# A 128-column stationary operand for attention times value, in a kernel of cosine attention and a highway layer

## The chip, the cores and the metric

The kernel runs on one NeuronCore of one Trainium2 chip. The metric is the device time of one execution in microseconds, the median of the runs shown. A profile of one execution comes with it; its span runs from the first to the last instruction.

## What is computed

Inputs are q, k and v of shape (8, 12, 448, 64) in fp32: 8 batches, 12 heads, 448 positions, 64 columns. Attention is by cosine: q and k are divided by their norms.

```python
scores = np.matmul(q_n, k_n.transpose(0, 1, 3, 2)) / tau      # tau = 0.1
attn = softmax(scores)
attn_out = np.matmul(attn, v)
x = attn_out.transpose(0, 2, 1, 3).reshape(3584, 768)
H = np.maximum(x @ w_h, 0.0)
T = 1.0 / (1.0 + np.exp(-(x @ w_t + b_t)))
out = T * H + (1.0 - T) * x
```

## The kernel before

S = 448 positions are cut into NC = 4 chunks of P = 112, so most tiles use 112 of 128 partitions. Everything is written for one batch at a time, with pairs of heads (NPAIR = 6) as the unit of loading.

**Preparing a pair.** `emit_A` loads q and k of two heads (L92) through the SyncE queue, squares them on GpSimd (`qk_sq`, L97) and sums the squares on VectorE (L104). `emit_rsqrt` makes the inverse norms on VectorE. `emit_B` multiplies q and k by them on GpSimd (`qkn`, L152, two instructions a pair), transposes the result on TensorE (`qkT`, L157, eight transposes of 112x128 blocks, so the stationary operand is 128 columns wide and the moving identity 112), copies the transposes to SBUF on VectorE (L164), loads v (L168), writes the column of twos that gives the softmax's sum (a GpSimd memset of 112x8, L173) and converts v to fp16 on ScalarE (L174). `vp` is 65 columns wide per head: 64 of v and that one.

**Scores.** `emit_qkt(b, pr, g)` multiplies k chunks by q for two heads at a time (L186, 64 rows, 448 moving columns) into PSUM and takes the exponential on ScalarE (L194, 112x896) into `expt`. Called for g = 0 and 1, it fills, for each head, a tile `expt` of [128, 4, 448] fp16: chunk jc of the keys lies on the partitions, the 448 queries along the row. The pool of `expt` has four buffers, one a head.

**Attention times value.** `emit_av(b, h)` (L201 to L227) makes, for each of four query chunks ic, four accumulating matmuls over jc (L208): the stationary operand is `expt[:P, jc, ic*P:(ic+1)*P]`, 112x112, the moving one `vp[:P, jc, hh]`, 112x65, the output `u[:P, ic, 0:65]` in PSUM. That is 16 pairs of weight load and matmul a head, 96 heads, 1536 pairs. VectorE then takes the reciprocal of the sums (L219) and scales the rows into `xb` (L220).

**The highway layer of the batch before** is spread over the heads of the present one by `ffn_slot`: TensorE transposes `xb` (`xTp`, L234, also with 128-column stationary operands), VectorE copies (L240), TensorE multiplies with w_h and w_t (`pt`, L255, 112-column stationary operand and 384 moving columns) and adds the bias (L263), ScalarE takes tanh (L271), VectorE combines (L274, L291, L299), and SyncE's queue stores the output (L307).

**Order.** The kernel is written with a tile framework. The lines say which engine does what; the framework orders each engine's instructions at compile time by a priority that follows the order of the program (some copies out of PSUM are moved ahead by 300), places tiles in the pools' buffers and sets the semaphores. Each engine then runs its list in order. In the main loop (L330 to L347), head h of batch b comes with the loads of pair h of batch b+1 for h below 6, with the two `expt` tiles and the scores for even h, then `emit_av`, then a slot of the highway layer of b-1, then `emit_B` of batch b+1 for h from 6 on. All of batch 0 is prepared ahead of the loop, and the last batch's highway layer follows it.

Of the kernel before, what the change touches and what calls it, by code (L numbers as in the profile page):

```python
# [10 lines left out]
FP16 = mybir.dt.float16  # L11
# [7 lines left out]
def kernel(  # L19
# [11 lines left out]
    nc = tc.nc  # L31

    B, NH, S, D = q.shape
    P = 112
    NC = S // P
# [17 lines left out]
    expt_p = ctx.enter_context(tc.tile_pool(name="expt", bufs=4))  # L53
# [33 lines left out]
    st = {}  # L87

    def emit_A(b, pr):
        qk_raw = qkraw_p.tile([128, 2, NC, 2, D], FP32, name="qk_raw")  # L90
        for t, src in enumerate((q, k)):
            nc.sync.dma_start(  # L92
                qk_raw[:P, t],
                src[b, 2 * pr : 2 * pr + 2].rearrange("h (p c) d -> p c h d", c=NC),
            )
        qk_sq = qksq_p.tile([128, 2, NC, 2, D], FP16, name="qk_sq")
        nc.gpsimd.tensor_mul(qk_sq[:P], qk_raw[:P], qk_raw[:P])  # L97

        if pr == 0:
            n2 = nrm_p.tile([128, NPAIR, 2, NC, 2], FP16, name="n2")  # L100
            st["n2", b] = n2
        n2 = st["n2", b]
        with nc.allow_low_precision(reason="norm^2 in fp16 (rel err 5e-4)"):
            nc.vector.reduce_sum(n2[:P, pr], qk_sq[:P], axis=AX.X)  # L104
        st["qk_raw", b, pr] = qk_raw

    def emit_rsqrt(b, prs=None):
        n2 = st["n2", b]
        NE = NPAIR * 2 * NC * 2
        if prs is None:  # L110
            if ("rs", b) not in st:
                st["rs", b] = nrm_p.tile([128, NE], FP32, name="yy")
            x32 = nrm_p.tile([128, NE], FP32, name="x32")
            yy = st["rs", b]
            tt_ = nrm_p.tile([128, NE], FP32, name="tt_")
            n2s = n2[:P].opt()
        else:
            if ("rs", b) not in st:
                st["rs", b] = nrm_p.tile([128, NE], FP32, name="yy")
            NE = 16  # L120
            x32 = nrm_p.tile([128, NE], FP32, name="x32p")
            yy = st["rs", b][:, prs * 16 : (prs + 1) * 16]
            tt_ = nrm_p.tile([128, NE], FP32, name="tt_p")
            n2s = n2[:P, prs].opt()
        nc.vector.tensor_copy(x32[:P], n2s)
        nc.vector.tensor_single_scalar(
            yy[:P].bitcast(I32), x32[:P].bitcast(I32), 1, ALU.arith_shift_right
        )
        nc.vector.tensor_scalar(
            out=yy[:P].bitcast(I32),  # L130
            in0=yy[:P].bitcast(I32),
            scalar1=-1.0,
            scalar2=float(0x5F3759DF),
            op0=ALU.mult,
            op1=ALU.add,
        )
        for _ in range(2):
            nc.vector.tensor_mul(tt_[:P], yy[:P], yy[:P])
            nc.vector.tensor_mul(tt_[:P], tt_[:P], x32[:P])
            nc.vector.tensor_scalar(  # L140
                out=tt_[:P], in0=tt_[:P], scalar1=-0.5, scalar2=1.5,
                op0=ALU.mult, op1=ALU.add,
            )
            nc.vector.tensor_mul(yy[:P], yy[:P], tt_[:P])  # L144

    def emit_B(b, pr):
        qk_raw = st.pop(("qk_raw", b, pr))
        rs = st["rs", b].rearrange("p (pr t c h) -> p pr t c h", pr=NPAIR, t=2, c=NC)
        qkn = qkn_p.tile([128, 2, NC, 2, D], FP16, name="qkn")
        for t in range(2):  # L150
            in1 = rs[:P, pr, t].unsqueeze(3).to_broadcast([P, NC, 2, D])
            nc.gpsimd.tensor_mul(qkn[:P, t], qk_raw[:P, t], in1)  # L152

        qkT = pb1_p.tile([128, 2, 512], FP16, name="qkT", tag="pb1")
        for t in range(2):
            for c in range(NC):
                nc.tensor.transpose(  # L157
                    qkT[:, t, c * P : (c + 1) * P],
                    qkn[:P, t, c],
                    ident[:P, :P],  # L160
                )
        qkt = qt_p.tile([128, 2, S], FP16, name="qkt")
        with tc.high_priority(offset=300):
            nc.vector.tensor_copy(qkt[:, :, :], qkT[:, :, 0:S])  # L164
        st["qkt", b, pr] = qkt

        v_raw = vraw_p.tile([128, NC, 2, D], FP32, name="v_raw")
        nc.sync.dma_start(  # L168
            v_raw[:P],
            v[b, 2 * pr : 2 * pr + 2].rearrange("h (p c) d -> p c h d", c=NC),  # L170
        )
        vp = vp_p.tile([128, NC, 2, D + 1], FP16, name="vp")
        nc.gpsimd.memset(vp[:P, :, :, D], 2.0)  # L173
        nc.scalar.copy(vp[:P, :, :, 0:D], v_raw[:P])  # L174
        st["vp", b, pr] = vp

    def emit_qkt(b, pr, g):
        qkt = st["qkt", b, pr]
        sTs = []
        for hh in range(2):  # L180
            sT = sT_p.tile([128, 2, 512], FP32, name="sT", tag="sT")
            sTs.append(sT)
        for jj in range(2):
            jc = 2 * g + jj
            for hh in range(2):
                nc.tensor.matmul(  # L186
                    sTs[hh][:P, jj, 0:S],
                    lhsT=qkt[hh * D : (hh + 1) * D, 1, jc * P : (jc + 1) * P],
                    rhs=qkt[hh * D : (hh + 1) * D, 0, 0:S],
                    start=True,  # L190
                    stop=True,
                )
        for hh in range(2):
            nc.scalar.activation(  # L194
                st["expt", b, 2 * pr + hh][:P, 2 * g : 2 * g + 2, :],
                sTs[hh][:P, :, 0:S],
                AF.Exp,
                scale=inv_tau,
            )

    def emit_av(b, h):  # L201
        pr, hh = h // 2, h % 2
        vp = st["vp", b, pr]
        expt = st["expt", b, h]
        u = pb1_p.tile([128, NC, 128], FP32, name="u", tag="pb1")
        for ic in range(NC):
            for jc in range(NC):
                nc.tensor.matmul(  # L208
                    u[:P, ic, 0 : D + 1],
                    lhsT=expt[:P, jc, ic * P : (ic + 1) * P],  # L210
                    rhs=vp[:P, jc, hh],
                    start=(jc == 0),
                    stop=(jc == NC - 1),
                )

        xb = st["xb", b]
        with tc.high_priority(offset=300):
            rd = nrm_p.tile([128, NC], FP32, name="rd")
            nc.vector.reciprocal(rd[:P, :], u[:P, :, D])  # L219
            nc.vector.scalar_tensor_tensor(  # L220
                out=xb[:P, pr, :, hh, :],
                in0=u[:P, :, 0:D],
                scalar=0.0,
                in1=rd[:P, :].unsqueeze(2).to_broadcast([P, NC, D]),
                op0=ALU.bypass,
                op1=ALU.mult,
            )  # L227
# [81 lines left out]
    def new_batch_tiles(b):  # L309
        xb = xb_p.tile([128, NPAIR, NC, 2, D], FP16, name="xbach")  # L310
        xT = xt_p.tile([128, CC, S], FP16, name="xTb")
        st["xb", b] = xb
        st["xT", b] = xT
# [8 lines left out]
    def ffn_slot(bprev, h):  # L322
        for qi in range(h * 16 // NH, (h + 1) * 16 // NH):
            if qi % 4 == 0:
                emit_xt(bprev, qi // 4)
            emit_ffn_quarter(bprev, qi // 4, qi % 4)
            if qi % 4 == 3:
                emit_ffn_final(bprev, qi // 4)

    for b in range(B):  # L330
        for h in range(NH):
            pr, hh = h // 2, h % 2
            if b + 1 < B and h < NPAIR:
                emit_A(b + 1, h)
            if hh == 0:
                for h2 in (h, h + 1):
                    st["expt", b, h2] = expt_p.tile([128, NC, S], FP16, name="expt")
                emit_qkt(b, pr, 0)
                emit_qkt(b, pr, 1)
            emit_av(b, h)  # L340
            if b >= 1:
                ffn_slot(b - 1, h)
            if b + 1 < B and h >= NPAIR:
                if h == NPAIR:
                    emit_rsqrt(b + 1)
                    new_batch_tiles(b + 1)
                emit_B(b + 1, h - NPAIR)  # L347
# [6 lines left out]
_INS = ['q', 'k', 'v', 'tau', 'moe_w_h', 'moe_w_t', 'moe_b_t']  # L354
_OUTS = [((3584, 768), 'float32')]
#: Inputs that are plain numbers.
_NUMBERS = {'tau': 0.10000000149011612}


# [26 lines left out]
```

## Time and profile before

| what | value |
|---|---|
| runs (2) | 512.85 and 511.74 us, median 512.3 us |
| span of the profiled execution | 509.7 us |
| what lies around the span, against the median | 2.6 us |
| TensorE busy, matmuls | 412.6 us, 81% |
| TensorE busy, weight loads | 286.6 us, 56% |
| VectorE busy | 314.3 us, 62% |
| ScalarE busy | 226.1 us, 44% |
| GpSimd busy | 201.7 us, 40% |

The profiled execution's own total is not listed apart from these; its span is what the rows add up to, and the 2.6 us carry it to the median. PE is TensorE's matmuls, PEld its weight loads, which can run beside matmuls; DVE is VectorE, ACT ScalarE, POOL GpSimd, SP SyncE. Matmuls overlap in the pipeline, so their busy time is no measure of a full engine; a single matmul's duration includes its way through the array. The granted clock is 1.00 at 2.4 GHz and 0.50 at 1.2 GHz.

### The profile page before, as it was taken

The page shows a single profiled execution, that of the slowest core. Times are in us where ns is not written, and L with a number is a line of the kernel's source. Part 1 is how long each engine was busy: PE and PEld are TensorE (multiplying, and loading weights), DVE is VectorE, ACT ScalarE, POOL GpSimd, SP SyncE. Part 2 cuts the span into 40 slices and gives each one's busy share as a digit, 9 for nine tenths or more (in the row PEclk, how much of TensorE's full clock was granted, in tenths as well). Part 3 has the DMA queues.
Part 4 walks back from the last instruction along what each step waited for, and adds up shares of the span by engine and source line. Part 5 has one row for each costly group of instructions (what it writes and reads, how often), then busy time and mean ns, then how long its engine had stood idle before and what let it go on. Part 6 is the DMA issues. An engine that isn't in the chain of part 4 may idle for free.

```text
span 509.7 us, 8460 instructions
## 1 busy us (share of the span) xinstructions
PE 412.6 (81%) x3328; PEld 286.6 (56%) x3328; DVE 314.3 (62%) x661; ACT 226.1 (44%) x305; POOL 201.7 (40%) x198
## 2 busy tenths in 40 slices
PE   0545945988776979889878999989887999899995
PEld 0114604766554656557655666657564767575774
DVE  3655465458277675666777494938685455453574
ACT  1321441346335453354453473454546455644511
POOL 3663296723924276337170833282517030000000
PEclk9999999999967797677898797959897899797999
DMA  9960695725553157415551554255231221000012
GB/s 173 224 167 1 211 192 105 147 57 129 109 117 81 39 131 140 100 46 113 142 110 45 132 123 103 62 118 138 70 74 46 64 65 46 27 28 28 29 55 81
DMA packets 137033, 49.31 MB, mean 97 GB/s; under 512 B 131873, under 2 KB 131873, under 8 KB 136994
## 3 DMA queue, kind: packets, MB, share of 16 engines
q1 hardware_dynamic: 136994, 48.77, 42.9%
q8 instruction: 26, 0.43, 0.4%
q14 instruction: 13, 0.11, 0.1%
HBM read 37.75 MB, written 11.01 MB: 96 GB/s over the span
## 4 chain that ended last, share of the span: by engine, by line
PE 53%; DVE 23%; ACT 5%; POOL 5%; SPq 5%; DMA 4%; issue 3%; POOLq 0%; ACTq 0%
PE pt L255 24%; PE u L208 15%; PE sT L186 9%; DVE outst L299 6%; DVE th1a L291 6%; DVE n L104 4%; PE qkT L157 4%; POOL qkn L152 3%; ACT expt L194 3%; SPq L92 3%; DMA qk_raw<-in_k_dram 3%; ACT tt L271 2%; DMA qk_raw<-in_q_dram 2%; POOL qk_sq L97 2%; DVE xTb L240 1%
## 5 line engine op out<-in xcount | busy, mean ns | idle before, releaser
L194 ACT ACTIVATE expt<-sT 112x896 f16<-112x896 f32 x192 | 166.7, 916 | 96.5 <-PE sT L186 77.7
L208 PEld LDWEIGHTS <-expt 112*112 112x112 f16 x1536 | 115.5, 158 | 40.1 <-issue 17.4
L208 PE MATMUL u<-vp,expt 112*112 112x65 f16 x1536 | 121.5, 238 | 12.9 <-DVE xbach L220 9.2
L255 PEld LDWEIGHTS <-xTb 128*112 128x112 f16 x768 | 101.8, 145 | 47.8 <-DVE xTb L240 15.0
L152 POOL TENSOR_TENSOR qkn<-qk_raw,yy 112x512 f16<-112x512 f32 x96 | 99.7, 1068 | 72.4 <-DVE yy L144 37.7
L186 PE MATMUL sT<-qkt 64*112 64x448 f16 x384 | 104.3, 437 | 26.3 <-ACT expt L194 25.6
L97 POOL TENSOR_TENSOR qk_sq<-qk_raw 112x1024 f16<-112x1024 f32 x48 | 96.3, 2013 | 29.5 <-DMA qk_raw<-in_k_dram 23.3
L255 PE MATMUL pt<-w_h_f,xTb 128*112 128x384 f16 x384 | 100.0, 402 | 5.4 <-DVE xTb L240 4.4
L174 ACT CAST vp<-v_raw 112x512 f16<-112x512 f32 x48 | 29.8, 621 | 118.8 <-PE u L208 78.8
L255 PE MATMUL pt<-w_t_f,xTb 128*112 128x384 f16 x384 | 77.2, 330 | 0.4 <-DVE hmx L274 0.3
L104 DVE TENSOR_REDUCE n<-qk_sq 112x16 f16<-112x1024 f16 x48 | 58.0, 1211 | 26.2 <-POOL qk_sq L97 26.2
L291 DVE SCALAR_TENSOR_TENSOR th1a<-tt,hmx 112x384 f16<-112x384 f16 x64 | 51.1, 798 | 33.2 <-ACT tt L271 33.2
L157 PE MATMUL qkT<-ident,qkn 112*128 112x112 f16 x384 | 35.5, 247 | 44.2 <-POOL qkn L152 40.9
L186 PEld LDWEIGHTS <-qkt 64*112 64x112 f16 x384 | 31.2, 140 | 62.3 <-issue 55.4
L173 POOL MEMSET vp<- 112x8 f16 x48 | 6.9, 149 | 147.4 <-PE u L208 147.4
L274 DVE SCALAR_TENSOR_TENSOR hmx<-pt,xbach 112x384 f16<-112x384 f32 x64 | 35.2, 553 | 39.2 <-PE pt L255 39.2
L271 ACT ACTIVATE tt<-pt 112x384 f16<-112x384 f32 x64 | 31.4, 491 | 62.6 <-PE pt L263 62.0
L157 PEld LDWEIGHTS <-qkn 112*128 112x128 f16 x384 | 28.5, 116 | 54.5 <-POOL qkn L152 45.7
L219 DVE RECIPROCAL rd<-u 112x4 f32<-112x4 f32 x96 | 17.2, 179 | 55.3 <-PE u L208 54.4
L299 DVE SCALAR_TENSOR_TENSOR outst<-xbach,th1a 112x384 f32<-112x384 f16 x64 | 49.2, 769 | 1.0
L164 DVE COPY qkt<-qkT 128x896 f16<-128x896 f16 x48 | 29.8, 620 | 21.1 <-PE qkT L157 11.8
L220 DVE SCALAR_TENSOR_TENSOR xbach<-u,rd 112x256 f16<-112x256 f32 x96 | 40.3, 421 | 1.9
(55 smaller groups left out, 116.8 us busy)
## 6 DMA issues: line engine op xcount, KB each, us to landing
qk_raw<-in_q_dram SPq DMA_DIRECT2D x48, 224.0 KB, 4.4
qk_raw<-in_k_dram SPq DMA_DIRECT2D x48, 224.0 KB, 4.4
v_raw<-in_v_dram SPq DMA_DIRECT2D x48, 224.0 KB, 3.4
out_dram<-outst SPq DMA_DIRECT2D x32, 336.0 KB, 2.8
w_raw<-in_moe_w_h_dram SPq DMA_DIRECT2D x1, 2304.0 KB, 10.8
w_raw<-in_moe_w_t_dram SPq DMA_DIRECT2D x1, 2304.0 KB, 8.7
bt_raw<-in_moe_b_t_dram SPq DMA_DIRECT2D x1, 3.0 KB
```

The source lines that it names most:

```text
L97: nc.gpsimd.tensor_mul(qk_sq[:P], qk_raw[:P], qk_raw[:P])
L104: nc.vector.reduce_sum(n2[:P, pr], qk_sq[:P], axis=AX.X)
L152: nc.gpsimd.tensor_mul(qkn[:P, t], qk_raw[:P, t], in1)
L157: nc.tensor.transpose(qkT[:, t, c * P : (c + 1) * P], qkn[:P, t, c], ident[:P, :P],)
L186: nc.tensor.matmul(sTs[hh][:P, jj, 0:S], lhsT=qkt[hh * D : (hh + 1) * D, 1, jc * P : (jc + 1) * P], rhs=qkt[hh * D : (hh + 1) * D, 0, 0:S] ...
L194: nc.scalar.activation(st["expt", b, 2 * pr + hh][:P, 2 * g : 2 * g + 2, :], sTs[hh][:P, :, 0:S], AF.Exp, scale=inv_tau,)
L208: nc.tensor.matmul(u[:P, ic, 0 : D + 1], lhsT=expt[:P, jc, ic * P : (ic + 1) * P], rhs=vp[:P, jc, hh], start=(jc == 0), stop=(jc == NC - 1),)
L220: nc.vector.scalar_tensor_tensor(out=xb[:P, pr, :, hh, :], in0=u[:P, :, 0:D], scalar=0.0, in1=rd[:P, :].unsqueeze(2).to_broadcast([P, NC, D]),
L255: nc.tensor.matmul(pt[:P, :], lhsT=xT[:, cc, ic * P : (ic + 1) * P], rhs=w_f[:, cc, mh * MH : (mh + 1) * MH], start=(cc == 0), stop=(cc == ...
L271: nc.scalar.activation(tt[:P, mh], pt[:P, :], AF.Tanh)
L291: nc.vector.scalar_tensor_tensor(out=th1a[:P, mh], in0=tt[:P, mh], scalar=1.0, in1=hmx[:P, mh], op0=ALU.add, op1=ALU.mult,)
L299: nc.vector.scalar_tensor_tensor(out=outst[:P, mh * MH : (mh + 1) * MH], in0=xg, scalar=2.0, in1=th1a[:P, mh], op0=ALU.mult, op1=ALU.add,)
```

## The change

The `expt` tile becomes flat, [128, 4*448 + 16], and its last 16 columns are set to zero by a GpSimd memset when the tile is made. ScalarE writes the same elements through a rearranged view. The stationary operand of L208 is read 128 columns wide from where it began before, so it takes in the first 16 columns of what follows: the next query chunk, the next key chunk's row, or, for the last block, the pad. The output is `u[:, ic, 0:65]` on all 128 partitions; partitions 112 to 127 hold values that nothing reads.

```diff
             nc.scalar.activation(
-                st["expt", b, 2 * pr + hh][:P, 2 * g : 2 * g + 2, :],
+                st["expt", b, 2 * pr + hh][:P, 2 * g * S : (2 * g + 2) * S].rearrange(
+                    "p (j s) -> p j s", j=2
+                ),
                 sTs[hh][:P, :, 0:S],
...
                 nc.tensor.matmul(
-                    u[:P, ic, 0 : D + 1],
-                    lhsT=expt[:P, jc, ic * P : (ic + 1) * P],
+                    u[:, ic, 0 : D + 1],
+                    lhsT=expt[:P, jc * S + ic * P : jc * S + ic * P + 128],
                     rhs=vp[:P, jc, hh],
...
                 for h2 in (h, h + 1):
-                    st["expt", b, h2] = expt_p.tile([128, NC, S], FP16, name="expt")
+                    et = expt_p.tile([128, NC * S + 16], FP16, name="expt")
+                    nc.gpsimd.memset(et[:P, NC * S : NC * S + 16], 0.0)
+                    st["expt", b, h2] = et
```

## Rows read from the trace of the kernel before

**Rows 1.** The page, part 1: busy us, share of the span, instructions.

```profile
PE 412.6 (81%) x3328; PEld 286.6 (56%) x3328; DVE 314.3 (62%) x661; ACT 226.1 (44%) x305; POOL 201.7 (40%) x198
```

**Rows 2.** The page, part 4: the chain that ended last, by engine and line.

```profile
PE 53%; DVE 23%; ACT 5%; POOL 5%; SPq 5%; DMA 4%; issue 3%; POOLq 0%; ACTq 0%
...
by line: PE pt L255 23.9%; PE u L208 15.4%; PE sT L186 8.7%; DVE outst L299 6.1%; DVE th1a L291 6.1%; DVE n L104 3.8%; PE qkT L157 3.6%; POOL qkn L152 3.4%; ACT expt L194 3.4%; SPq L92 3.3%; issue 3.2%; DMA qk_raw<-in_k_dram 2.5%; ACT tt L2
```

**Rows 3.** Timeline, TensorE, 287 to 313: start us, us, engine, instruction, count.

```profile
287.49 1.67 PE L208 MATMUL u<-vp,expt 112*112 112x65 f16 x16
...
290.05 0.97 PE L208 MATMUL u<-vp,expt 112*112 112x65 f16 x16
...
309.26 0.95 PE L157 MATMUL qkT<-ident,qkn 112*128 112x112 f16 x8
...
313.24 0.56 PE L157 MATMUL qkT<-ident,qkn 112*128 112x112 f16 x8
```

**Rows 4.** Busy time by window around these groups; after POOL, the granted clock.

```profile
287.49:289.10 1.61, 1.61 (x18) 1.61 (x17) 0.56 (x1) 0.00 (x0) 1.61 (x2) 0.50 0.04 4
290.05:291.00 0.95, 0.95 (x18) 0.95 (x17) 0.95 (x2) 0.00 (x0) 0.95 (x1) 1.00 0.00 0
309.30:310.20 0.90, 0.90 (x12) 0.90 (x11) 0.56 (x1) 0.00 (x0) 0.00 (x0) 0.50 0.00 0
313.30:313.70 0.40, 0.40 (x9) 0.34 (x7) 0.26 (x1) 0.00 (x0) 0.00 (x0) 1.00 0.00 0
```

**Rows 5.** Instructions of L208, L157, L173: duration ns min/median/max, first and last start.

```profile
L208 PE MATMUL u<-vp,expt x1536: 195/218/303, 45.8 to 481.4; 112*112 112x65 f16 x192
...
L157 PE MATMUL qkT<-ident,qkn x384: 210/213/302, 15.5 to 434.8; 112*128 112x112 f16 x192
...
L173 POOL MEMSET vp<- x48: 127/133/912, 0.9 to 451.4; 112x8 f16 x48
```

**Rows 6.** Groups by line: busy us, mean ns, idle before and releaser.

```profile
L194 ACT ACTIVATE expt<-sT 112x896 f16<-112x896 f32 x192 | 166.7, 916 | 96.5 <-PE sT L186 77.7 <-PE u L208 17.6
...
L208 PEld LDWEIGHTS <-expt 112*112 112x112 f16 x1536 | 115.5, 158 | 40.1 <-issue 17.4 <-DVE xbach L220 10.8 <-PE sT L186 3.0
...
L255 PEld LDWEIGHTS <-xTb 128*112 128x112 f16 x768 | 101.8, 145 | 47.8 <-DVE xTb L240 15.0 <-issue 9.5
L152 POOL TENSOR_TENSOR qkn<-qk_raw,yy 112x512 f16<-112x512 f32 x96 | 99.7, 1068 | 72.4 <-DVE yy L144 37.7 <-PE qkT L157 31.0 <-DMA qk_raw<-in_q_dram 3.6
L97 POOL TENSOR_TENSOR qk_sq<-qk_raw 112x1024 f16<-112x1024 f32 x48 | 96.3, 2013 | 29.5 <-DMA qk_raw<-in_k_dram 23.3 <-DVE outst L299 2.7 <-DVE th1a L291 1.9
...
L157 PEld LDWEIGHTS <-qkn 112*128 112x128 f16 x384 | 28.5, 116 | 54.5 <-POOL qkn L152 45.7 <-DVE xbach L220 3.2 <-issue 2.0
...
L234 PEld LDWEIGHTS <-xbach 112*128 112x128 f16 x192 | 12.5, 110 | 10.9 <-issue 6.5 <-DVE xbach L220 4.0
```

**Rows 7.** Timeline, the start of the group at 290.05, cut after one and two matmuls.

```profile
290.05 0.20 PE L208 MATMUL u<-vp,expt 112*112 112x65 f16 x1
...
290.05 0.25 PE L208 MATMUL u<-vp,expt 112*112 112x65 f16 x2
```

**Rows 8.** Waits: engine, line, waited for; us in total, times, longest.

```profile
POOL vp L173 <- PE u L208: 147.4, 30, 13.2
...
DVE rd L219 <- PE u L208: 54.4, 55, 3.2
```

**Rows 9.** Timeline, GpSimd from 280.46 and VectorE from 301.83.

```profile
280.46 7.04 POOL L152 TENSOR_TENSOR qkn<-qk_raw,yy 112x512 f16<-112x512 f32 x7
...
301.83 0.56 DVE L291 SCALAR_TENSOR_TENSOR th1a<-tt,hmx 112x384 f16<-112x384 f16 x1 [0.43 <-ACT tt L271]
302.43 0.56 DVE L299 SCALAR_TENSOR_TENSOR outst<-xbach,th1a 112x384 f32<-112x384 f16 x1
302.97 0.56 DVE L291 SCALAR_TENSOR_TENSOR th1a<-tt,hmx 112x384 f16<-112x384 f16 x1
303.57 2.13 DVE L299 SCALAR_TENSOR_TENSOR outst<-xbach,th1a 112x384 f32<-112x384 f16 x1
```

**Rows 10.** Span and mean granted clock of the core.

```profile
core 0: 509.7 us, clock 0.887
```

## Prediction

> **What bounds the kernel now.** I read the busy shares first, then the chain that ended last, then the groups by line, and at the end single matmul groups in the timeline. TensorE is busy for 81% of the span, VectorE for 62%, ScalarE for 44% and GpSimd for 40% [rows 1]. The reader should not take 81% for a full engine, since overlapping matmuls count there; the chain says more. Of the chain 53% is TensorE work and 23% VectorE work, and its second largest line is the attention-times-value matmul, `u` at L208, with 15.4% of the span [rows 2]. 15.4% of 509.7 us is 78.5 us. So this line is on the path that sets the end for most of its life, mixed with the highway matmuls of L255 (23.9%).
>
> What sets the pace inside L208 is the load, not the matmul. At the full clock (1.00, 2.4 GHz) a group of 16 pairs goes from 290.05 for 0.97 us [rows 3, 4]; the last matmul itself lasts 0.218 us [rows 5], so the 15 steps between starts take (0.97 - 0.218)/15 = 50.1 ns. The moving operand has 65 columns, 27.1 ns at 2.4 GHz; the stationary one has 112, 46.7 ns. The step is 112 columns plus 3.4 ns. At the half clock (0.50, 1.2 GHz) a group at 287.49 takes 1.67 us [rows 3, 4], its last matmul up to 0.30 [rows 5]: with 0.28 the step is (1.67 - 0.28)/15 = 93 ns, where 112 columns are 93.3 ns and 65 are 54.2. Both say: each pair waits for its 112-column load, while the moving part would be done in 0.58 of the time.
>
> **The wider load.** The change makes the stationary operand 128 columns wide in all 1536 pairs. The trace of before has 128-column loads on other lines: the transposes at L157 and L234. Their loads last 116 and 110 ns on average, although they are wider; the 112-column ones last 158 (L208) and 145 ns (L255) [rows 6]. A group of eight transposes at full clock takes 0.56 us [rows 3], the last one 0.213 [rows 5]: (0.56 - 0.213)/7 = 49.6 ns a pair, which is its 112 moving columns (46.7 ns) plus 2.9. A 128-column load at one column per cycle would be 53.3 ns and could not fit into that step. At half clock eight transposes take 0.95 us [rows 3], the last up to 0.30 [rows 5]: (0.95 - 0.30)/7 = 93 ns, again the 112 moving columns, where such a load would be 106.7. So on this chip a load of exactly 128 columns is quicker than one of 112 and hides wholly behind 112 moving columns. The Trainium skill ("TensorE: Matmul & The Clock Gate", section "Weight-path perf modes — Fast Weight Load (FWL) and DoubleRow") states that a fast mode switches on when there are exactly 128 weights of a type other than FP32; the trace agrees as far as those 116 and 110 ns go. The same page (section "LDWEIGHTS (loading the stationary operand)") states the rule that speaks against the change: the load's time is its columns divided by 1.2 GHz, so 128 would cost 14% more than 112. By that rule the step would be 57 ns; the transposes' 49.6 ns disagrees.
>
> Bounds for the new step: it can't be under the 65 moving columns, 27.1 ns at full clock, and the nearest sustained row is the transposes' 49.6 ns. Between them lies one hint: behind a highway matmul, which hides the first loads, one matmul of L208 ends after 0.20 us and the first two together after 0.25 [rows 7]; since the second lasts about as long as the others (0.218), it started only some 0.03 to 0.04 us after the first. I take 27.1 plus the transposes' 2.9, so 30 ns; at half clock 54. Both are 0.58 to 0.60 of now, so the clock need not be known to size the term: 0.40 x 78.5 us = 31.4 us on the chain.
>
> **How much of it stays.** After a group, VectorE takes the reciprocal (L219) and the scaling (L220). In 55 of the 96 groups VectorE sat idle until `u` was ready, 54.4 us in all, 1.0 us each [rows 8]; a group that is 16 x 20 ns = 0.32 us shorter (0.62 at half clock) is passed on in full there. In the other 41 VectorE came late, and only the matmuls queued on TensorE gain. 55/96 = 57% is the lower end, 100% the upper; I take the middle, 78%: 24.5 us. What is late next is VectorE: around 301.8 to 305.7 it runs th1a, outst, th1a, outst without a pause, and one of these ops takes 2.13 us instead of 0.56 when GpSimd works beside it [rows 9].
>
> **The memsets.** 96 memsets of 112x16 are added on GpSimd; the nearest row, 112x8 at L173, has 133 ns as its median and 0.91 us as its longest [rows 5]. 96 x 0.133 = 12.8 us of GpSimd time. GpSimd sat idle 147.4 us waiting for L208 alone [rows 8], so the work itself is hidden; without that cover it would be 12.8 us. If each one held up VectorE for as long as it runs, VectorE's 23% of the chain would make 2.9 us of it; below nothing there is no way to gain. I take 1.5 us. Each memset must also wait until the buffer (one of four, so the head four earlier) has been read by TensorE, and the 16th pair of each group now waits for the memset, as it reads the pad. Behind a waiting memset stand the squares (L97, 2.0 us) and the normalising multiplies (L152, 1.07 us) of the next batch [rows 6], which TensorE's transposes wait for. ScalarE's exponentials wait for the same buffer and take 4 x 0.92 us per pair of heads [rows 6] before the last matmul can go, so I cost this wait at nothing; its price stands under the rivals.
>
> **Views, output rows, clock.** The flat exponentials tile and the AP rearranged for ScalarE have the same 112x896 shape: nothing. `u` is written in 128 partitions instead of 112; only 112 are read, and the matmul's time goes by its columns: nothing. The clock is 0.887 on average [rows 10], so (1 - 0.887)/0.5 = 23% of the span, 115 us, stands at half. TensorE may pause more often (clock down) or stream more densely in each stretch (clock up). If a tenth of the 115 us changed level, at 53% of the chain and a factor of two, it is 11.5 x 0.53 x 0.5 = 3 us either way. I take 1.5 us of gain, since the moving columns stay the same and the time shrinks; it cancels the memsets.
>
> **The sum.** 509.7 - 24.5 + 1.5 - 1.5 = 485.2 us of span; the median of the runs, 512.3, lies 2.6 us above the span, so 487.8; I say 488 us, 4.8% faster. About 2%, 10 us, is what a measurement of this kernel tells from no change.
>
> **Rivals.** (A) The pairs can't be issued faster than the transposes show. For it: 49.6 ns is the shortest step that any long group in the trace keeps. Against: the early second matmul [rows 7]. Then 50.1 becomes 49.6 and the time stays at 512. The Trainium skill ("TensorE: Matmul & The Clock Gate", section "Back-to-back issue gap") gives about 81 ns per pair of load and 128-column matmul as the sustained rate; the 49.6 ns here, at 112 columns, is already well under it. Chance 0.10.
> (B) The gain is taken up by VectorE and ScalarE: only a third of the 31.4 us stays, 502 us and up. For it: VectorE holds 23% of the chain and its two-tile ops stretch beside GpSimd [rows 2, 9]. Against: the 55 idle waits [rows 8]. Chance 0.08 for a result within 2%.
> (C) The memset becomes TensorE's wait: GpSimd works in order, and if a memset stands behind one multiply of L152, the last matmul of a pair waits 1.07 us. 48 pairs x 1.07 = 51 us against 24.5 gained: 512.3 + 27 = 539. It decides from 24.5/48 = 0.51 us per pair. For it: around 280.46 GpSimd runs seven such multiplies in a row, 7.04 us [rows 9]. Against: its 147.4 us of waiting for L208 show it ahead of TensorE nearly everywhere. Chance 0.07.
> (D) The wide load goes by its columns: step 57 ns, 78.5 x 16/112 = +11 us, 523. Only the transposes speak to it, and against it. Chance 0.03.
>
> **How the numbers follow.** The forecast has 0.72. Its own range is 475 to 498: all 31.4 us plus some clock at one end, 57% of it less the memsets' worst at the other. The range of 8 in 10 goes from 468 to 511. At the low end all 31.4 us stay and 13 more come from the clock, somewhat under half of what the half clock costs on the chain now (115 x 0.53 x 0.5 = 30 us). The high end takes in B but leaves out A, C and D, together 0.20. Faster by over 2%: the forecast, 0.72. Within 2%: A and B, 0.18. Slower: C and D, 0.10.
>
> **What would show it.** In the profile after, a 16-pair group at full clock should take about 0.67 us (15 x 30 + 218 ns) and the mean load of L208 should fall from 158 to about 115 ns; L208's share of the chain should go from 15% to about 9%. If the group stays at 0.97, A or D is right. If TensorE shows waits for a GpSimd memset of `expt`, C is. If the groups shrink but VectorE's share of the chain grows past 30%, B is. I am wrong if the step falls and the time does not.

## The result and the profile after

The changed kernel takes 488.5 us, the median of 487.2 and 489.8, against 512.3. The ratio is 0.9525 with a 95% interval of 0.9447 to 0.9603: faster by about 24 us. The forecast was 488 us. The span of the profiled execution is 485.1 us; 485.2 had been added up. The sum came out right; at least one of its terms, the memsets, did not, and the experiments below show it. A ratio with an interval compares only the quicker executions of each kernel, while times are medians of all runs, so the two can differ by some us where the kernel before had few such executions (the second and third sets below).

The same rows of the kernel after, beginning with the page's busy line and the chain (these answer to [rows 1, 2]; lines below L208 have moved, so L208 is now L210, L255 is L257, L291 is L293):

```profile
PE 369.8 (76%) x3328; PEld 240.3 (50%) x3328; DVE 309.2 (64%) x661; ACT 225.6 (47%) x305; POOL 206.4 (43%) x294
...
PE 46%; DVE 24%; POOL 12%; ACT 6%; issue 6%; DMA 4%; SPq 0%; POOLq 0%; ACTq 0%
PE pt L257 24%; PE sT L186 9%; PE u L210 9%; POOL qkn L152 8%; DVE th1a L293 6%; DVE outst L301 5%; DVE n L104 5%; POOL qk_sq L97 5%; DMA qk_raw<-in_k_dram 4%; ACT expt L194 4%; PE qkT L157 3%; ACT tt L273 2%; DVE xTb L242 2%; PE pt L265 1%; DVE qkt L164 1%
```

The reader is to see that `u` fell from 15.4% of 509.7 us to 9% of 485.1 us, that is from 78 to about 43 us, while GpSimd's share of the chain grew from 5% to 12%. The chain spends 47 us less on TensorE and 33 us more on GpSimd, and SyncE's queue, 5% before, is no longer on it. (GpSimd's share grows nearly as much without memsets, as the load alone shows below.)

The groups themselves, in the timeline of the kernel after, one at full and one at half clock, and then the windows that give their clock (these answer to [rows 3, 4]):

```profile
162.25 1.04 PE L210 MATMUL u<-vp,expt 112*128 112x65 f16 x16 [2.26 <-DVE qkt L164]
...
284.21 0.66 PE L210 MATMUL u<-vp,expt 112*128 112x65 f16 x16
```

```profile
284.25:284.80 0.55, 0.55 (x18) 0.55 (x17) 0.55 (x2) 0.00 (x0) 0.04 (x1) 1.00 0.00 0
162.25:163.20 0.95, 0.95 (x16) 0.88 (x15) 0.00 (x0) 0.00 (x0) 0.00 (x0) 0.50 0.75 217
```

The instructions of these lines (min/median/max in ns, as in [rows 5]), and the groups by line with their means (as in [rows 6]):

```profile
L210 PEld LDWEIGHTS <-expt x1536: 94/98/153, 45.3 to 456.7; 112*128 112x128 f16 x192
L210 PE MATMUL u<-vp,expt x1536: 190/196/263, 45.4 to 456.8; 112*128 112x65 f16 x192
...
L340 POOL MEMSET expt<- x96: 103/111/1581, 1.0 to 445.1; 112x16 f16 x96
```

```profile
L210 PE MATMUL u<-vp,expt 112*128 112x65 f16 x1536 | 80.2, 210 | 16.1 <-DVE xbach L222 12.5 <-DVE qkt L164 3.1
...
L210 PEld LDWEIGHTS <-expt 112*128 112x128 f16 x1536 | 70.1, 108 | 46.2 <-issue 21.8 <-DVE xbach L222 15.2 <-ACT expt L194 2.6
...
L340 POOL MEMSET expt<- 112x16 f16 x96 | 11.5, 126 | 102.6 <-PE u L210 65.8 <-ACT expt L194 36.8
```

A group at full clock went from 0.97 to 0.66 us: (0.66 - 0.196)/15 = 30.9 ns a step, where it was 50.1. At half clock it went from 1.67 to 1.04: the step is between (1.04 - 0.263)/15 = 52 and (1.04 - 0.196)/15 = 56 ns, as the last matmul is taken at the line's longest or at its median, where it was 93. The 65 moving columns (27.1 and 54.2 ns) now set the step, and the load hides. The last row is easily misread: the memsets run for 11.5 us, and GpSimd stood idle 102.6 us in front of them, waiting for TensorE and ScalarE to give the buffer back. Most of that is no new waiting, as the next rows show.

The waits (as in [rows 8]) and the granted clock (as in [rows 10]):

```profile
POOL expt L340 <- PE u L210: 65.8, 27, 7.4
...
POOL vp L173 <- PE u L210: 42.9, 21, 6.2
...
DVE rd L221 <- PE u L210: 28.5, 40, 2.6
...
DVE n L104 <- POOL expt L340: 11.4, 2, 8.9
```

```profile
core 0: 485.1 us, clock 0.903
```

VectorE waits 28.5 us for `u` instead of 54.4, which fits a gain that is passed on. GpSimd waited 147.4 us in front of the small memset of L173 [rows 8]; it now waits 42.9 there and 102.6 in front of the new ones, 145.5 together. So what counts is not how long it waits, but what stands behind it where it does. A new pair has come as well: the reduction of the squares (L104) waited twice, 8.9 us the longest, for a memset. That longest wait ends at 140 us and costs nothing: from head 6 of batch 1 to head 0 of batch 2 this kernel takes 38.1 us, and 38.5 with no memsets in the loop (the fixed tiles below).

The order of the instructions on TensorE, VectorE, ScalarE and SyncE's queue is the same before and after; only GpSimd's list differs, by the 96 memsets and a few places where they moved its neighbours. So the whole difference is in durations and waits.

### The profile page after: what moved, and what is told of

The parts are those of the page before. It is cut to its first block, busy times and chain, and to the rows that moved or that the text cites. A ratio compares the mean times of both kernels' runs of the same rounds, so it can differ in the third digit from the quotient of the medians.

```text
span 485.1 us, 8592 instructions
## 1 busy us (share of the span) xinstructions
PE 369.8 (76%) x3328; PEld 240.3 (50%) x3328; DVE 309.2 (64%) x661; ACT 225.6 (47%) x305; POOL 206.4 (43%) x294
## 4 chain that ended last, share of the span: by engine, by line
PE 46%; DVE 24%; POOL 12%; ACT 6%; issue 6%; DMA 4%; SPq 0%; POOLq 0%; ACTq 0%
PE pt L257 24%; PE sT L186 9%; PE u L210 9%; POOL qkn L152 8%; DVE th1a L293 6%; DVE outst L301 5%; DVE n L104 5%; POOL qk_sq L97 5%; DMA qk_raw<-in_k_dram 4%; ACT expt L194 4%; PE qkT L157 3%; ACT tt L273 2%; DVE xTb L242 2%; PE pt L265 1%; DVE qkt L164 1%
## 5 line engine op out<-in xcount | busy, mean ns | idle before, releaser
L257 PEld LDWEIGHTS <-xTb 128*112 128x112 f16 x768 | 100.4, 143 | 58.7 <-DVE xTb L242 23.6
L257 PE MATMUL pt<-w_h_f,xTb 128*112 128x384 f16 x384 | 97.5, 394 | 14.4 <-DVE xTb L242 14.1
L97 POOL TENSOR_TENSOR qk_sq<-qk_raw 112x1024 f16<-112x1024 f32 x48 | 94.1, 1968 | 29.2 <-DMA qk_raw<-in_k_dram 21.7
L210 PEld LDWEIGHTS <-expt 112*128 112x128 f16 x1536 | 70.1, 108 | 46.2 <-issue 21.8
L210 PE MATMUL u<-vp,expt 112*128 112x65 f16 x1536 | 80.2, 210 | 16.1 <-DVE xbach L222 12.5
L104 DVE TENSOR_REDUCE n<-qk_sq 112x16 f16<-112x1024 f16 x48 | 58.1, 1212 | 40.6 <-POOL qk_sq L97 29.2
L257 PE MATMUL pt<-w_t_f,xTb 128*112 128x384 f16 x384 | 77.1, 329 | 3.3 <-DVE hmx L276 3.1
L157 PE MATMUL qkT<-ident,qkn 112*128 112x112 f16 x384 | 35.2, 244 | 46.2 <-POOL qkn L152 43.6
L293 DVE SCALAR_TENSOR_TENSOR th1a<-tt,hmx 112x384 f16<-112x384 f16 x64 | 48.9, 764 | 28.6 <-ACT tt L273 28.3
L273 ACT ACTIVATE tt<-pt 112x384 f16<-112x384 f32 x64 | 31.4, 491 | 61.6 <-PE pt L265 61.6
L157 PEld LDWEIGHTS <-qkn 112*128 112x128 f16 x384 | 27.4, 113 | 57.0 <-POOL qkn L152 49.1
L340 POOL MEMSET expt<- 112x16 f16 x96 | 11.5, 126 | 102.6 <-PE u L210 65.8
L301 DVE SCALAR_TENSOR_TENSOR outst<-xbach,th1a 112x384 f32<-112x384 f16 x64 | 45.7, 715 | 1.0
L164 DVE COPY qkt<-qkT 128x896 f16<-128x896 f16 x48 | 29.8, 620 | 21.6 <-PE qkT L157 13.3
L221 DVE RECIPROCAL rd<-u 112x4 f32<-112x4 f32 x96 | 17.0, 177 | 28.5 <-PE u L210 28.5
```

The lines of the kernel that those rows point to most:

```text
L157: nc.tensor.transpose(qkT[:, t, c * P : (c + 1) * P], qkn[:P, t, c], ident[:P, :P],)
L210: nc.tensor.matmul(u[:, ic, 0 : D + 1], lhsT=expt[:P, jc * S + ic * P : jc * S + ic * P + 128], rhs=vp[:P, jc, hh], start=(jc == 0), stop= ...
L257: nc.tensor.matmul(pt[:P, :], lhsT=xT[:, cc, ic * P : (ic + 1) * P], rhs=w_f[:, cc, mh * MH : (mh + 1) * MH], start=(cc == 0), stop=(cc == ...
L273: nc.scalar.activation(tt[:P, mh], pt[:P, :], AF.Tanh)
L293: nc.vector.scalar_tensor_tensor(out=th1a[:P, mh], in0=tt[:P, mh], scalar=1.0, in1=hmx[:P, mh], op0=ALU.add, op1=ALU.mult,)
L301: nc.vector.scalar_tensor_tensor(out=outst[:P, mh * MH : (mh + 1) * MH], in0=xg, scalar=2.0, in1=th1a[:P, mh], op0=ALU.mult, op1=ALU.add,)
```

## The experiments

The kernels of a set share a chip and the runs of the kernel before; the three sets ran on different chips. The first set has the changed kernel again, the pads alone, the load alone, and a half.

**The changed kernel again.**

> The changed kernel once more, beside the others on one chip. All theories: 488 us within its interval (486 to 490), ratio to before 0.95.

487.9 us, ratio 0.9524 (0.947 to 0.9578). The base for the next three.

**The pads alone.**

```diff
-                    u[:, ic, 0 : D + 1],
-                    lhsT=expt[:P, jc * S + ic * P : jc * S + ic * P + 128],
+                    u[:P, ic, 0 : D + 1],
+                    lhsT=expt[:P, jc * S + ic * P : jc * S + (ic + 1) * P],
```

> The flat tile and the 96 memsets alone; the stationary operand stays 112 columns wide. Theory 1 (the whole gain is the quick load, the memsets are hidden): 511 to 515 us, the 16-pair group at full clock stays at 0.97 us. Theory 2 (the memsets cost several us, since GpSimd waits in them for TensorE and ScalarE while squares and multiplies stand behind, and the wide load's gain is larger than 24 us): 518 to 525 us.

515.0 us against 511.9, ratio 1.0089 (1.0049 to 1.0129). The medians are 3.1 us apart; the ratio makes it 4.6 us, 2.5 to 6.6 by the interval. 515.0 is the upper end of theory 1's range, but the memsets aren't hidden: by the ratio they cost three times the 1.5 us I had put down. The group at full clock stays as it was, by the timeline:

```profile
275.65 0.97 PE L210 MATMUL u<-vp,expt 112*112 112x65 f16 x16
```

**The load alone.** No pad and no memset; the last of the 16 pairs stays narrow.

```diff
-                    et = expt_p.tile([128, NC * S + 16], FP16, name="expt")
-                    nc.gpsimd.memset(et[:P, NC * S : NC * S + 16], 0.0)
-                    st["expt", b, h2] = et
+                    st["expt", b, h2] = expt_p.tile([128, NC * S], FP16, name="expt")
...
+                w = P if ic == NC - 1 and jc == NC - 1 else 128
                 nc.tensor.matmul(
-                    u[:, ic, 0 : D + 1],
-                    lhsT=expt[:P, jc * S + ic * P : jc * S + ic * P + 128],
+                    u[:w, ic, 0 : D + 1],
+                    lhsT=expt[:P, jc * S + ic * P : jc * S + ic * P + w],
```

> The wide load without pad and memsets: 15 of 16 pairs read 128 columns, the last (ic = 3, jc = 3) reads 112. Theory 1: 15/16 of 24 us, so 488 to 491 us. Theory 2: the memsets' cost goes, 476 to 483 us. The 16-pair group should be some 0.02 us longer than in the changed kernel.

486.3 us, ratio 0.9496 (0.9448 to 0.9543), its order that of the kernel before on every engine. It lies 1.6 us under the changed kernel, within both intervals, and just below the 488 to 491 us of theory 1: by this set alone theory 1 looks right, and the third set below measures it again. Its chain by engine:

```profile
PE 42%; DVE 26%; POOL 11%; issue 5%; DMA 5%; ACT 5%; SPq 4%; POOLq 0%; ACTq 0%
```

GpSimd holds 11% of the chain here, as against 12% with memsets and 5% before. So its larger share goes with the shorter groups and does not need the memsets.

**Half of the heads.**

```diff
+        w = 128 if hh == 0 else P
...
-                    u[:, ic, 0 : D + 1],
-                    lhsT=expt[:P, jc * S + ic * P : jc * S + ic * P + 128],
+                    u[:w, ic, 0 : D + 1],
+                    lhsT=expt[:P, jc * S + ic * P : jc * S + ic * P + w],
```

> 128 columns for the even heads only, 112 for the odd ones; tile and memsets as in the changed kernel. Theory 1 in its simple form (each shortened group hands on the same part): half of the gain, 499 to 501 us. Rival 3 (the gain saturates, because VectorE, ScalarE and GpSimd become the bound): most of it comes with the first half, 490 to 495 us. A clock that rises only when all groups are dense would give the opposite, 503 us or more.

494.9 us, ratio 0.9675 (0.9627 to 0.9722): 20.2 us under the pads alone, of 27.2 for all heads. The simple form of theory 1 falls. Either the gain saturates, or even heads are worth more than odd ones; the counterpart was to tell.

> The counterpart of the half kernel: 128 columns for the odd heads, 112 for the even ones. Even heads alone brought 20.2 of the 27.2 us between the pads-only kernel (515.0) and the changed one (487.9). If the gain saturates whichever half is quick, odd heads bring about as much: 494 to 498 us. If each head has its own worth and they add up, odd heads bring the remaining 7 us: 506 to 510 us.

501.5 us (499.7 to 505.4), while the kernel before stood at 513.7. It lies 12.2 us under the kernel before, where the even heads alone lay 17.0 under theirs. Against the pads alone, 515.0 on the other chip, the odd heads bring 13.5 us; with that kernel's 3.1 us added to the 513.7 of this chip, 15.3. Neither is one of the two numbers expected. Both things hold: an even head is worth more, and the two halves add up to 34 to 36 us where all heads bring 27, so 6 to 8 us are lost when both are quick. What takes them these runs don't show.

**120 columns.**

```diff
-                    u[:, ic, 0 : D + 1],
-                    lhsT=expt[:P, jc * S + ic * P : jc * S + ic * P + 128],
+                    u[:120, ic, 0 : D + 1],
+                    lhsT=expt[:P, jc * S + ic * P : jc * S + ic * P + 120],
```

> The stationary operand is read 120 columns wide instead of 128; tile and memsets as in the changed kernel. Theory 1 (only a load of exactly 128 columns is quick, any other goes by its columns): the step at full clock is 120/2.4 + 3.4 = 53.4 ns, a 16-pair group 1.02 us, the time that of the pads-only kernel (515.0) plus 78.5 x 8/112 x 0.8 = 4 us, so 517 to 522 us. Rival (a wider read is quicker step by step, or what helps is the output on all partitions): a group below 0.97 us and a time below 512 us.

517.5 us (512.4 to 523.0), in the lower half of what was expected, beside 513.7 for the kernel before. Four runs with that spread don't tell it from the pads alone; the group does. Timeline of the 120-column kernel, and its window with the clock:

```profile
295.98 1.02 PE L210 MATMUL u<-vp,expt 112*120 112x65 f16 x16
...
299.13 1.02 PE L210 MATMUL u<-vp,expt 112*120 112x65 f16 x16
```

```profile
299.20:300.10 0.90, 0.90 (x20) 0.90 (x19) 0.90 (x2) 0.49 (x1) 0.00 (x0) 1.00 1.01 170
```

With its median matmul of 221 ns the step is (1.02 - 0.221)/15 = 53.3 ns, as expected to a tenth, and longer than the 50.1 of 112 columns. So the step goes by the load's columns at 112 and at 120, and at 128 it drops to 30.9 ns. The Trainium skill ("TensorE: Matmul & The Clock Gate", section "Weight-path perf modes — Fast Weight Load (FWL) and DoubleRow") names exactly 128 weights as the condition; the two groups here agree.

**A quick load with a long step.** The moving operand takes 47 columns of the neighbouring head along, which nothing reads.

```diff
+        M = 112
+        c0 = 0 if hh == 0 else 2 * (D + 1) - M
+        o = hh * (D + 1) - c0
...
-                    u[:, ic, 0 : D + 1],
+                    u[:, ic, 0:M],
...
-                    rhs=vp[:P, jc, hh],
+                    rhs=vp[:P, jc].rearrange("p h d -> p (h d)")[:, c0 : c0 + M],
```

> The quick 128-column load stays, but the moving operand is 112 columns wide (the head's 65 columns and 47 of its neighbour, which nothing reads), so that the step should be the transposes' 49.6 ns at full clock and 93 at half. The framework orders some instructions otherwise with it. If only the step counts: 510 to 520 us, about the pads-only kernel's 515. If the quick load is worth something in itself: below 500 us.

512.8 us (507.7 to 517.3) beside 513.3 for the kernel before, ratio 1.0054 (0.9976 to 1.0132). Its groups at full clock, from its timeline, and its load by line:

```profile
298.33 0.95 PE L213 MATMUL u<-vp,expt 112*128 112x112 f16 x16
```

```profile
L213 PEld LDWEIGHTS <-expt 112*128 112x128 f16 x1536 | 98.7, 110 | 48.7 <-issue 29.6 <-DVE xbach L225 7.4 <-ACT expt L194 6.4
```

The load is as quick as in the changed kernel (110 ns on average, 108 there), the step, with this line's median matmul of 212 ns, is (0.95 - 0.212)/15 = 49.2 ns, and the gain is gone. So the gain comes from the shorter step; a quick load behind a long step brings nothing that can be seen. The framework orders part of the instructions otherwise here, on TensorE, VectorE and ScalarE as well, so a few us either way could come from that.

**Who takes the rest?** The next two ask whether VectorE does: both leave out the factor of the tanh. With that line gone the framework orders instructions on every engine otherwise than in the kernel before, and alike in these two, so they are compared with each other.

```diff
-            nc.vector.scalar_tensor_tensor(
-                out=th1a[:P, mh],
-                in0=tt[:P, mh],
-                scalar=1.0,
-                in1=hmx[:P, mh],
-                op0=ALU.add,
-                op1=ALU.mult,
-            )
...
-                in1=th1a[:P, mh],
+                in1=hmx[:P, mh],
```

> The kernel before with less work on VectorE: the instruction at L291 (th1a, 64 times 0.8 us, 51 us) is left out, and the output is made from hmx without the tanh factor. Its loads are 112 wide, no memsets. VectorE holds 23% of the chain, and this line 6.1% (31 us): 480 to 500 us by every theory. It is the base for the next kernel.

> The same lighter kernel with 15 of 16 loads 128 wide and no memsets; the order on all engines is that of the lighter narrow kernel. With the full VectorE work the same step brought 25.6 us (511.9 to 486.3). If VectorE takes up the missing part of the 37 us of shorter matmul streams, it brings 30 us or more here. If GpSimd, ScalarE or the pauses of TensorE itself take it up, it brings 25 us or less.

491.9 us (487.9 to 494.3) narrow and 464.9 us (461.6 to 467.9) wide: 27.1 us, against 25.6 and, in the third set, 30.9 with VectorE's full work. It lies between the two numbers expected (30 or more, 25 or less). The chains of the two by engine, narrow and then wide:

```profile
PE 57%; DVE 12%; POOL 10%; DMA 6%; ACT 5%; SPq 5%; issue 4%; POOLq 0%; ACTq 0%
```

```profile
PE 44%; DVE 18%; POOL 15%; DMA 7%; issue 6%; SPq 5%; ACT 4%; POOLq 0%; ACTq 0%
```

VectorE's share of the chain is 12% and 18% here, where it was 23% before and 26% with the load alone, and the gain lies within the two that were measured with its full work. So nothing shows that VectorE holds back the missing part; the two measurements with full work are 5 us apart, so a few us of it can't be excluded.

**No memsets in the loop, all loads wide.** The exponentials lie in four fixed tiles, padded once. The order stays that of the kernel before but for the memsets and a few places on ScalarE, where neighbours change over.

```diff
+    expt_fix = [
+        const.tile([128, NC * S + 16], FP16, name=f"expt{i}") for i in range(4)
+    ]
+    for et in expt_fix:
+        nc.gpsimd.memset(et[:P, NC * S : NC * S + 16], 0.0)
...
-                    et = expt_p.tile([128, NC * S + 16], FP16, name="expt")
-                    nc.gpsimd.memset(et[:P, NC * S : NC * S + 16], 0.0)
-                    st["expt", b, h2] = et
+                    st["expt", b, h2] = expt_fix[h2 % 4]
```

> All 16 loads 128 wide, but the exponentials lie in four fixed tiles whose pads are zeroed once at the start, so the 96 memsets in the loop are gone. Pads alone cost 4.6 us (515.0 against 511.9). If the memsets' waits cost that much beside the quick load too: 483 to 485 us and a ratio of 0.943 to 0.948. If the cost is given back elsewhere once the groups are short: 487 to 489 us, as the changed kernel.

> The kernel without pad and memsets, 15 of 16 loads wide, once more for a narrower comparison: 485 to 488 us, ratio 0.947 to 0.953, by both theories within 2 us of the changed kernel.

> The changed kernel beside these two on one chip: 486 to 490 us, ratio 0.950 to 0.955.

| kernel, third set | median, us | extremes, us |
|---|---|---|
| before | 513.3 | 504.1 to 515.8 |
| changed | 489.8 | 485.4 to 492.9 |
| load alone, 15 of 16 | 482.5 | 480.0 to 485.0 |
| fixed tiles, 16 of 16 | 480.7 | 479.1 to 488.4 |

The fixed tiles have the best median of the four; the load alone is 1.8 us away, which these runs can't tell apart. The ratios to the kernel before are 0.9451 (0.9366 to 0.9535) for the fixed tiles, 0.9484 (0.9399 to 0.9568) for the load alone and 0.9609 (0.9466 to 0.9752) for the changed kernel. Against what was expected, the fixed tiles and the load alone are quicker in us and inside by ratio (the first theory's for the fixed tiles); the changed kernel is inside in us and above its range by ratio. Every run of the load alone lies under every run of the changed kernel. The size of the memsets' cost beside the quick load stays loose, 2 us in the first set and 7 to 9 in this one, and in the profiles it has one main place. The timelines below give the start of the group of head 0 and of head 6 of batch 1, in the kernel before, with the pads alone, in the changed kernel (third set) and with the fixed tiles (the last two begin with head 6 of batch 0):

```profile
99.76 0.40 PE L208 MATMUL u<-vp,expt 112*112 112x65 f16 x2
...
123.91 0.29 PE L208 MATMUL u<-vp,expt 112*112 112x65 f16 x2
```

```profile
99.13 0.40 PE L210 MATMUL u<-vp,expt 112*112 112x65 f16 x2
...
126.43 0.29 PE L210 MATMUL u<-vp,expt 112*112 112x65 f16 x2
```

```profile
58.00 0.40 PE L210 MATMUL u<-vp,expt 112*128 112x65 f16 x4
...
96.26 0.35 PE L210 MATMUL u<-vp,expt 112*128 112x65 f16 x3
...
124.76 0.24 PE L210 MATMUL u<-vp,expt 112*128 112x65 f16 x2
```

```profile
58.43 0.29 PE L215 MATMUL u<-vp,expt 112*128 112x65 f16 x2
...
96.58 0.46 PE L215 MATMUL u<-vp,expt 112*128 112x65 f16 x5
...
118.15 0.23 PE L215 MATMUL u<-vp,expt 112*128 112x65 f16 x2
```

From head 0 to head 6 it takes 24.2 us before, 27.3 with pads alone, 28.5 in the changed kernel and 21.6 with fixed tiles. The memsets cost 3 us there with slow groups, by one profile each, and 7 with quick ones. In all three profiles of the changed kernel the stretch takes 26.5 to 28.5 us, in the load alone's two and the fixed tiles' one 19.9 to 21.6. (Elsewhere part of it comes back: from head 6 of batch 3 to head 0 of batch 4 the load alone takes 29.5 and 32.4 us, the changed kernel 26.4 to 26.7.) GpSimd, VectorE and TensorE of the changed kernel in this stretch say why, from their timelines:

```profile
106.35 0.11 POOL L340 MEMSET expt<- 112x16 f16 x1 [2.05 <-PE u L210]
106.50 1.89 POOL L97 TENSOR_TENSOR qk_sq<-qk_raw 112x1024 f16<-112x1024 f32 x1
...
109.27 4.06 POOL L97 TENSOR_TENSOR qk_sq<-qk_raw 112x1024 f16<-112x1024 f32 x2
```

```profile
108.42 1.22 DVE L104 TENSOR_REDUCE n<-qk_sq 112x16 f16<-112x1024 f16 x1 [1.54 <-POOL qk_sq L97]
109.56 2.02 DVE L293 SCALAR_TENSOR_TENSOR th1a<-tt,hmx 112x384 f16<-112x384 f16 x1
...
111.61 2.13 DVE L301 SCALAR_TENSOR_TENSOR outst<-xbach,th1a 112x384 f32<-112x384 f16 x1
...
114.55 2.17 PE L257 MATMUL pt<-w_h_f,xTb 128*112 128x384 f16 x6 [4.74 <-DVE xTb L242]
```

And with the fixed tiles in the same place:

```profile
107.53 0.55 DVE L298 SCALAR_TENSOR_TENSOR th1a<-tt,hmx 112x384 f16<-112x384 f16 x1
...
108.23 0.53 DVE L306 SCALAR_TENSOR_TENSOR outst<-xbach,th1a 112x384 f32<-112x384 f16 x1
...
108.36 4.32 POOL L102 TENSOR_TENSOR qk_sq<-qk_raw 112x1024 f16<-112x1024 f32 x2
...
109.56 1.18 PE L262 MATMUL pt<-w_h_f,xTb 128*112 128x384 f16 x6 [0.66 <-DVE xTb L247]
```

A memset waits 2.05 us for TensorE, a square stands behind it and starts late, VectorE's reduction waits 1.54 us for the square, and the next two instructions of VectorE then fall beside the following squares and take 2.02 and 2.13 us, where without the memset they begin before those squares do and take 0.55 and 0.53. TensorE's highway matmuls wait for VectorE in turn, 4.74 us instead of 0.66, and the six after that pause run at a granted clock of 0.50 and take 2.17 us instead of 1.18 at 1.00.

## Why the prediction was right

**The step.** 30 ns at full clock and 54 at half were forecast; 30.9 and 52 to 56 were measured. The group was to take 0.67 us and took 0.66; the mean load was to fall to about 115 ns and fell to 108; the share of the chain was to go to about 9% and did, from 78 to some 43 us, a little more than the 31.4 us forecast. Rivals A (issue) and D (time by columns) are both out by the 30.9 ns; the 120 columns show that D's rule does hold there, at 53.3 ns, and stops at 128. Rival B's sign, VectorE past 30% of the chain, did not show: it has 24%. The 81 ns a pair that the Trainium skill ("TensorE: Matmul & The Clock Gate", section "Back-to-back issue gap") gives for 128 moving columns is far above the steps measured here, 49.6 with 112 and 30.9 with 65, and the measurement decides.

**How much of it stays: about right or too small.** I let 78% of 31.4 us through, 24.5, and gave the clock 1.5, so 26.0 us without memsets; a measured gain holds both. The load alone, 15 of 16 pairs, brought 25.6 us in the first set (23 to 28 by the interval). In the third set it brought 30.9 us by the medians and about 26 by its ratio, and the fixed tiles, all pairs, 32.7 and about 28. So the term was right or up to 7 us too small, and these runs don't settle which. I had named VectorE as the taker of the rest; the lighter kernels don't bear that out. A stretch where nothing passes can be seen in the rows above. From head 6 of batch 0 to head 0 of batch 1 the kernel before takes 38 us, the changed one 38.3 (58.00 to 96.26) and the fixed tiles 38.2 (58.43 to 96.58), although each of the six groups is 0.6 us shorter. The three longest pieces of the changed kernel's chain (from the first profile, where head 6 starts at 58.08) begin there or shortly ahead of it, and they are loads and GpSimd:

```profile
53.49 9.95 DMA qk_raw<-in_k_dram
63.50 3.12 POOL qk_sq L97
67.11 5.21 DMA qk_raw<-in_k_dram
78.64 4.71 POOL qkn L152 x5
86.78 3.07 POOL qkn L152 x4
```

Six times 0.6 us, 3.6 in all, are lost there. It isn't the only such stretch: from head 6 to the next head 0 the kernel before takes 39.3, 30.5 and 30.1 us in batches 1, 4 and 5, and the fixed tiles 38.5, 29.6 and 30.9. How much is missing in total stays open: against 31.4 us the measured 25.6 to 32.7 leave anything from 6 us to nothing.

**The memsets: too cheap, and the step that failed is the wait.** I took 1.5 us, and priced at nothing the wait for a buffer, on the ground that ScalarE waits for the same buffer. The pads alone cost 4.6 us (2.5 to 6.6) by the ratio, 3.1 by the medians; beside the quick load it was 1.6 us in the first set and 7 to 9 in the third. The ground was right for TensorE, which never waits for a memset in the profile after; but the price lay with what is queued behind the waiting memset, the squares, which I had named and not costed. Rival C is out as it stands: its sign, TensorE waiting for a memset of `expt`, did not show, and no 51 us came, since GpSimd is ahead of TensorE almost everywhere. The price is one stretch of 3 to 7 us, by way of the squares and VectorE.

**The clock.** 0.887 became 0.903, so by these means the time at half level went from (1 - 0.887)/0.5 x 509.7 = 115 to (1 - 0.903)/0.5 x 485.1 = 94 us. The reading behind that was incomplete. The profile gives 1.00 for the whole of the first 108 us before (104 after), yet the groups of L208 there last as long as elsewhere at 0.50, as this one of the kernel before with its window:

```profile
61.74 1.70 PE L208 MATMUL u<-vp,expt 112*112 112x65 f16 x16
...
61.74:63.40 1.66, 1.66 (x19) 1.60 (x18) 0.00 (x0) 0.92 (x1) 1.30 (x1) 1.00 1.14 303
```

So more than 115 us ran at the slow pace. The sign came as forecast, but no run shows the 1.5 us or the reason given for it; what the clock brought is contained in the numbers above and could not be measured apart.

The mechanism was right: the step, its cause and its size. That the span came out within 0.1 us of the sum is luck. The memsets' wait, priced at nothing, was too cheap by some us in all but one of the comparisons, and what came through of the shorter step made up for it.

## What to carry to other kernels

Where a stationary operand has a little under 128 columns (112 here, in fp16) and the moving operand is shorter than it, look at the step inside a group of matmuls: if it follows the stationary columns, padding to exactly 128 is worth the trouble, and padding to 120 is not. Make the padding once, in tiles that stay, and not in each turn of the loop. An instruction that runs 0.1 us still holds a whole in-order queue while it waits for its buffer, so cost what stands behind it.

## What the runs showed of the hardware

A weight load of 120 columns sets a step of 53.3 ns at full clock and one of 128 columns lets the step go down to 30.9 ns, with 65 moving columns: wider and quicker. A pair of load and matmul can follow the last one after 30.9 ns in groups of 16; no long group in the trace before had kept a step shorter than 49.6. VectorE's two-tensor instructions at L293 and L301, 0.55 us alone, took 2.0 and 2.1 beside GpSimd's squares, and so a wait of 2 us ended in a stretch that was 7 us longer. And the granted clock that the profile gives for a kernel's start can be wrong: 1.00 stood beside groups of 1.70 us, which take 0.97 at 1.00 later.
